# Attention with two mixture layers: row scaling on two engines, a branch ahead of the row loads, full-width transposes

## The chip, the cores and the metric

The kernel runs on one core of a Trainium2 chip. A core has TensorE (PE, matrix products, its weight loads listed as PEld), VectorE (DVE), ScalarE (ACT), GpSimd (POOL) and SyncE (SP, which here only issues DMAs and reads registers). The metric is the device time of one execution in microseconds (us).

## The reference

Three layers follow one another on B = 4, H = 8, S = 576, D = 64 (2304 tokens, 512 channels):

```python
scores = scale * np.matmul(q, k.transpose(0, 1, 3, 2))
bias = -(cum[:, :, :, None] - cum[:, :, None, :])          # cum: running sum of max(s, 0)
scores = np.where(causal, -1000000000.0, scores + np.minimum(bias, 0.0))
attn = softmax(scores);  x = attn @ v                       # to 2304 x 512
...
logits = xn @ en.T / tau;  expert_idx = np.argmax(logits, axis=1)   # 8 experts, normed rows
out[mask] = gate_w[mask, None] * (np.maximum(x[mask] @ w1[e], 0.0) @ w2[e])   # 512 -> 1024 -> 512
...
return (x @ w_a) * (x @ w_b) @ w_out                        # 512 -> 1536 -> 512
```

## The kernel before

**Attention (0 to 262 us).** The 32 heads are worked in units. A planner, class `Sched` (object `V`), keeps a time for each of four engines (P, A, D, G) and a heap of follow-up operations; `run` takes, among several streams of PE items, the one that can start first by the planner's costs, emits its matmuls, and `push` and `chain` put the evictions, maxima, exponentials and copies on the engines. Where `push` names two engines it takes the one that would end first. The order that results is fixed in the program. The streams are the scores (`s_item`, `s0_item`), transposes of the exponentials (`t_item`), products with v (`a_item`), and, per tile of 128 tokens, `x_item`, `l_item` and `r_item`. There are 20 tiles, five per batch; the last one (t = 19) has 64 tokens.

`x_item` multiplies attention's output by the router's embedding (L857, tile `lp`, logits with experts in rows), and transposes it into rows of tokens (L862, tile `pt`); DVE scales the rows by the reciprocal row sums (`fx`, L895, into `x`), ACT squares them (`fs`, L902, into `ss`), and the logits are copied to `lt`. `l_item` transposes `lt` back (L930), DVE finds the largest (L938 to L953) and makes the one-hot row `oh` (L956), and GpSimd keeps a running sum `sc` (L961). `r_item` gets each token's rank within its expert by products of `oh` with a triangle (L982) and of `sc` with ones (L983), and GpSimd scatters the rows to the sorted buffer `xs` by indirect DMA (L1004).

**Handover.** The counts are summed on PE (L1250), copied (L1257), sorted on DVE and written as integers to `ci` (L1274). Then come base offsets (L1276 to L1281), twelve operations that split three loaded weight tiles into a high and a low half (`hi_op` on ACT, `lo_op` on DVE, L280), and the gate's pieces m1 to m4 (L1443 to L1458) on DVE. SP, having waited for all scatters, loads the first expert's rows (`xload(0)`, L1332 and L1333, tile `xg`) and a weight tile (`wload2`, L242). PE runs 30 warm-up matmuls on a weight tile (L174, count in `WARM[2]`). All engines then read the number of tokens above capacity from `ci` (L1719) and branch around `overflow()` (L1661), which serves experts above their capacity and is not entered with these counts. `xtr0` transposes the rows (L1345); ACT makes `xh`, DVE `xl` (L1349).

**Experts (about 273 to 500 us).** The eight experts stand in order of their counts, with fixed capacities 352, 368, 344, 328, 296, 288, 288, 272. For each f of eight, PE makes `h` (L1510) from `xh` and `xl` and `y` (L1535) from the split `hh` and `hl` (L1518, L1519). `xtr` transposes the next expert's rows, a third of them m = capacity - 256 wide (L1361). The results go to `yt` (L1547); `yload` (L1580) reads 384 of its columns for the last layer, `ysplit` splits them (L1587, L1588).

**Last layer (about 500 us to the end).** Six groups of 384 tokens; `abmm` (L1600), `omm` (L1621). Its weights arrive as 64-bit values, decoded on ACT, DVE (L254 to L265) and split (L1431, L1433) in steps called ticks.

Of the kernel before, what the change touches and what calls it, by code (L numbers as in the profile page):

```python
# [35 lines left out]
WARM = (30, 84, 30, 0, 20, 28)  # L36
# [108 lines left out]
def moe_kernel(tc, q, k, v, s, emb, tau, w1, w2, wa, wb, wo, out, dbg=None):  # L145
# [36 lines left out]
    with left, right:  # L182
# [23 lines left out]
        ci = rt.tile([1, 5, E], I32, name="ci")  # L206
        tie = rt.tile([128, E], F32, name="tie")
# [80 lines left out]
        if True:  # L288
# [293 lines left out]
            def start(i):  # L582
# [84 lines left out]

            def s0_item(i):
# [12 lines left out]
                def emit(end):  # L681
# [22 lines left out]
                    def th1(t):  # L704
                        rel.t = t
                        V.push(t, "A", 0.833 * 64 + 280, f2, lambda t2: setattr(et, "t", t2))
# [132 lines left out]

            def x_item(b, c):  # L840
# [11 lines left out]
                def emit(end):  # L852
# [3 lines left out]
                    for p in range(NP):  # L856
                        nc.tensor.matmul(  # L857
                            lp[32 * p:32 * p + 32, :m], lhsT=enbd[:, p].rearrange("p h e -> p (h e)"),
                            rhs=xtt[4 * b + p][:, s0:s0 + m], start=True, stop=True,
                        )  # L860
# [5 lines left out]
                    r = sm.tile([128, H], F32, name="r")  # L866
                    lt = sm2.tile([128, 128], F32, name="lt")
# [8 lines left out]
                    def f0a(_):  # L876
                        if c:
                            nc.vector.tensor_scalar(out=r[:m], in0=rsum[:m, t, :], scalar1=1e-9, scalar2=None, op0=ALU.add)
                        for h in range(0 if c else 2):
                            nc.vector.tensor_scalar(  # L880
                                out=r[:m].rearrange("p (a h) -> p a h", h=2)[:, :, h],
                                in0=rsum0[64 * h:64 * h + 64, NP * b:NP * b + NP],
                                scalar1=1e-9, scalar2=None, op0=ALU.add,
                            )
# [7 lines left out]
                    V.push(end - 400, "DA", (dt(m), at(m)), f0, th)  # L892
# [10 lines left out]

                    def thx(t_):
                        rel.t = t_
                        V.push(t_, "A", 620, fs)

                    rk_ = rtok[t] = Tok()

                    def thr(t_):  # L910
                        rk_.t = t_
                        V.push(max(t_, end), "D", dt(512), fx, thx)
# [7 lines left out]
            def l_item(b, c):  # L920
# [6 lines left out]
                def emit(end):  # L927
                    x, r, lt = rts[t]
                    lp = ps_t.tile([128, 512], F32, name="pt")
                    nc.tensor.transpose(out=lp[:m, :128], in_=lt[:, :m], identity=ident)  # L930
                    rel = Tok()
                    pts.append(rel)
# [898 lines left out]
```

## Time and profile before

| | |
|---|---|
| median of three runs | 963.38 us (962.12 to 964.65) |
| profiled execution | 960.65 us, of which 959.0 are the profile's span |
| PE busy | 925.7 us, 97% of the span |
| PEld, DVE, ACT, POOL busy | 846.6, 514.6, 432.8, 255.1 us |
| data moved | 107.90 MB, mean 113 GB/s |

The profile's chain of work that ended last lies on PE for 66% of the span, on DVE and on DMA for 2% each. PE's pieces are pipelined and their ends are modelled, so how close PE is to its limit is read from the distance of starts, not from its share.

### The profile page before, as it was taken

The page shows a single profiled execution, that of the slowest core. Times are in us where ns is not written, and L with a number is a line of the kernel's source. Part 1 is how long each engine was busy: PE and PEld are TensorE (multiplying, and loading weights), DVE is VectorE, ACT ScalarE, POOL GpSimd, SP SyncE. Part 2 cuts the span into 40 slices and gives each one's busy share as a digit, 9 for nine tenths or more (in the row PEclk, how much of TensorE's full clock was granted, in tenths as well). Part 3 has the DMA queues.
Part 4 walks back from the last instruction along what each step waited for, and adds up shares of the span by engine and source line. Part 5 has one row for each costly group of instructions (what it writes and reads, how often), then busy time and mean ns, then how long its engine had stood idle before and what let it go on. Part 6 is the DMA issues. An engine that isn't in the chain of part 4 may idle for free.

```text
span 959.0 us, 17720 instructions
## 1 busy us (share of the span) xinstructions
PE 925.7 (97%) x6471; PEld 846.6 (88%) x6472; DVE 514.6 (54%) x1319; ACT 432.8 (45%) x1075; POOL 255.1 (27%) x311
## 2 busy tenths in 40 slices
PE   8999999999889999999999999999999999999996
PEld 7777778777779999999998999999999999999995
DVE  8688889798764334444558888742222212222112
ACT  6677788876745444455544444432211211211111
POOL 6122323256223333344302433642001001001001
PEclk9999999999999999999999999999999999999999
DMA  4774555526286667667645443613010010000000
GB/s 130 172 155 110 137 119 124 139 71 183 72 254 227 225 192 231 201 211 222 190 156 166 132 132 119 108 18 100 1 33 34 1 33 33 1 1 33 1 1 33
DMA packets 102243, 107.90 MB, mean 113 GB/s; under 512 B 58429, under 2 KB 72717, under 8 KB 102141
## 3 DMA queue, kind: packets, MB, share of 16 engines
q1 hardware_dynamic: 98557, 97.04, 36.2%
q0 software_dynamic: 3552, 9.46, 2.8%
q8 instruction: 65, 1.06, 0.5%
q14 instruction: 37, 0.30, 0.1%
q10 hardware_dynamic: 32, 0.04, 0.0%
HBM read 77.90 MB, written 20.44 MB: 103 GB/s over the span
## 4 chain that ended last, share of the span: by engine, by line
PE 66%; DVE 2%; DMA 2%; issue 1%; ACT 0%; POOL 0%; POOLq 0%; SPq 0%; DVEq 0%; ACTq 0%
PE h L1600 15%; PE x L1600 15%; PE y L1621 13%; PE h L1510 11%; PE y L1535 10%; PE x L1361 1%; DMA xg<-xs 1%; PE x L1621 1%; PE h L1621 1%; DMA xg<-yt 1%; DVE cv L262 0%; DVE cv L265 0%; DVE mx L1611 0%; DVE w L1433 0%; DVE xl L1588 0%
## 5 line engine op out<-in xcount | busy, mean ns | idle before, releaser
L1611 DVE TENSOR_TENSOR mx<-x,mx 128x384 f32<-128x384 f32 x72 | 40.0, 556 | 220.0 <-PE x L1600 220.0
L1612 ACT CAST hh<-mx 128x384 fp32r<-128x384 f32 x71 | 36.4, 513 | 161.1 <-DVE mx L1611 161.1
L1606 ACT COPY mx<-h 128x384 f32<-128x384 f32 x72 | 34.6, 481 | 144.1 <-PE h L1600 144.1
L650 ACT ACTIVATE z<-z,mn 128x192 f32<-128x192 f32 (+3 forms) x128 | 78.2, 611 | 37.8 <-DVE mn L644 37.2
L1640 POOL DMA_INDIRECT out_dram<-mx,pmt x18 | 17.6, 979 | 291.0 <-DVE mx L1639 221.7
L1600 PE MATMUL x<-xh,w 128*128 128x384 f32 x288 | 79.0, 335 | 1.0 <-POOL w L1433 1.0
L1600 PE MATMUL h<-xh,w 128*128 128x384 f32 x288 | 79.7, 337 | 0.0
L1600 PE MATMUL h<-xh,v 128*128 128x384 f32 x288 | 79.7, 337 | 0.0
L630 PE MATMUL st<-KS,QS 128*128 128x288 f32 (+3 forms) x160 | 58.6, 374 | 8.9 <-DVE mn L644 7.5
L738 PE MATMUL pt<-ident,z 128*128 128x128 f32 x448 | 63.4, 277 | 3.2 <-ACT pT L180 1.6
L1519 DVE SCALAR_TENSOR_TENSOR hl<-h,hh 128x288 fp32r<-128x288 f32 (+6 forms) x64 | 31.2, 488 | 65.1 <-ACT hh L1518 65.1
L280 POOL TENSOR_TENSOR w<-st,w 128x512 fp32r<-128x512 f32 (+1 forms) x41 | 44.5, 1093 | 74.2 <-ACT w L272 48.9
L644 DVE CUSTOM_DVE_ANT_0 z<-st,maskb 128x192 f32<-128x192 f32 (+3 forms) x128 | 58.7, 478 | 9.5 <-PE st L633 7.6
L782 PE MATMUL xa<-pT,vn 128*64 128x128 f32 x896 | 61.2, 282 | 0.8 <-ACT pT L180 0.4
L1613 DVE TENSOR_TENSOR hl<-mx,hh 128x384 fp32r<-128x384 f32 x71 | 39.7, 559 | 41.1 <-ACT hh L1612 41.1
L1621 PE MATMUL y<-v,hh 128*128 128x512 f32 x192 | 59.8, 392 | 0.0
L280 POOL TENSOR_TENSOR v<-st,v 128x512 fp32r<-128x512 f32 x32 | 42.9, 1341 | 63.3 <-ACT v L272 53.0
L738 PEld LDWEIGHTS pt<-ident,z 128*128 128x128 f32 x448 | 49.8, 141 | 11.0 <-ACT z L650 4.3
L1510 PE MATMUL h<-xh,v 128*128 128x256 f32 (+2 forms) x256 | 59.2, 305 | 0.0
L1510 PE MATMUL h<-xh,w 128*128 128x288 f32 (+3 forms) x256 | 58.9, 306 | 0.0
L1535 PE MATMUL y<-hh,v 128*128 128x256 f32 (+2 forms) x256 | 58.1, 300 | 0.0
L782 PEld LDWEIGHTS xa<-pT,vn 128*64 128x64 f32 x896 | 49.1, 139 | 9.9 <-issue 5.7
(299 smaller groups left out, 2525.7 us busy)
## 6 DMA issues: line engine op xcount, KB each, us to landing
st<-in_moe_w_dram SPq DMA_DIRECT2D x64, 512.0 KB
QS<-sp SPq DMA_DIRECT2D x62, 128.0 KB
st<-in_moe_w_a_dram SPq DMA_DIRECT2D x12, 512.0 KB
st<-in_moe_w_b_dram SPq DMA_DIRECT2D x12, 512.0 KB
st<-in_moe_w_out_dram SPq DMA_DIRECT2D x12, 512.0 KB
xg<-yt SPq DMA_DIRECT2D x6, 768.0 KB
xg<-xs SPq DMA_DIRECT2D x8, 512.0 KB
kn<-in_k_dram SPq DMA_DIRECT2D x24, 128.0 KB
```

Source lines behind the costliest of these rows:

```text
L280: e.tensor_tensor(out=o[:, 1, a:b], in0=t[:, a:b], in1=o[:, 0, a:b].bitcast(F32), op=ALU.subtract)
L630: nc.tensor.matmul(st[:m, :wp], lhsT=qs[:, h, s0 - 64:s0 - 64 + m], rhs=ks[:, h, c0:c0 + wp], start=True, stop=False)
L644: nc.vector.tensor_tensor_reduce(out=z[:m, h, c0:c0 + w], in0=st[:m, :w], in1=maskb[:m, S - kk + c0:S - kk + c0 + w], op0=ALU.add, op1=ALU ...
L650: nc.scalar.activation(out=z[:m, h, :kk], in_=z[:m, h, :kk], func=AF.Exp, scale=-1.0, bias=m1, accum_out=rsum[:m, tid(b, c), 2 * p + h:2 * ...
L738: nc.tensor.transpose(out=pt[:, 128 * x:128 * x + 128], in_=zs[i][:, h, a0:a0 + 128] if c else z0s[u % 2], identity=ident)
L782: nc.tensor.matmul(xa[64 * h:64 * h + 64, :m], lhsT=v_[:m, 2 * p + h, :], rhs=locs[i][bk, h], start=bk == 0, stop=bk == c,)
L1510: nc.tensor.matmul(ph[:, :n], lhsT=w[:, hl, 128 * f:128 * f + 128], rhs=mv[:, d, :n], start=k_ == 0, stop=k_ == 11,)
L1535: nc.tensor.matmul(ys[e][d][:, :n], lhsT=w[:, hl, c0 + 128 * d:c0 + 128 * d + 128], rhs=mv[:, :n], start=f == 0 and k_ == 0, stop=f == 7 a ...
L1600: nc.tensor.matmul(p, lhsT=w[:, hl, d, c0:c0 + 128], rhs=mv[:, d, :], start=d == 0 and k_ == 0, stop=d == 3 and k_ == 2,)
L1611: nc.vector.tensor_tensor(out=g, in0=pp[1], in1=g, op=ALU.mult)
L1613: nc.vector.tensor_tensor(out=gl, in0=g, in1=gh.bitcast(F32), op=ALU.subtract)
L1621: nc.tensor.matmul(ots[i][t], lhsT=st[:, 128 * t:128 * t + 128], rhs=w[:, hl, c0:c0 + 512], start=f == 0 and k_ == 0, stop=f == 11 and k_ ...
```

## The change

- The tiles of batches 0 to 2 may be scaled by DVE as before (`fx`), or copied by ACT (`fy`) and multiplied by GpSimd (`fm`); the planner picks. By the order of the program, 16 of the 20 scalings stay on DVE; of batch 1 and of batch 2 the 64-token tile and one of 128 tokens go the other way.
- The last tile's logits are computed with tokens in rows, so it has no `lt` copy and no transpose; its reciprocal (`rlast`) is made early, and its scaling comes behind its one-hot row.
- The running sum `sc` ends five tiles early; `r_item` and the final count add products of `oh` with ones in its place.
- `cov`, an integer copy of the overflow counts, is made right behind their maximum; branch and `overflow()` stand ahead of `xload(0)`, which is now three loads of at most 128 rows. One `wload2` goes ahead of the branch. The low halves of three weight tiles go behind it, a third of them on GpSimd. Of m1 to m4 two stay ahead of `xtr0`; base offsets go into m5.
- `WARM`: 30 matmuls ahead of the branch become 2 ahead and 3 behind, and 28 in the last `r_item` become 10.
- The third transpose of each row tile is always 128 x 128.
- `yload(0)` goes from the last expert's f = 1 to the f = 7 before; a tick is added in the last expert at f = 5, with fewer loads ahead from f = 4.
- The zeroing of the first rows of `xs` moves from a list of pending loads to a fixed place, unit step 14.

```diff
-WARM = (30, 84, 30, 0, 20, 28)
+WARM = (30, 84, 2, 0, 20, 10, 3)
...
+                if i == 14:
+                    zero(xs[:CAPS[0], :], 0)
...
+                        if t == NT - 1:
+                            nc.tensor.matmul(lp[:m, 32 * p:32 * p + 32], lhsT=xw, rhs=ew, start=True, stop=True)
+                        else:
+                            nc.tensor.matmul(lp[32 * p:32 * p + 32, :m], lhsT=ew, rhs=xw, start=True, stop=True)
...
+                    def fy(e):
+                        on[0] = e
+                        if e == "D":
+                            fx(e)
+                        else:
+                            nc.scalar.copy(out=x[:m], in_=pt[:m])
+
+                    def fm(_):
+                        nc.gpsimd.tensor_tensor(
+                            out=x[:m].rearrange("p (h d) -> p h d", h=H), in0=x[:m].rearrange("p (h d) -> p h d", h=H),
+                            in1=r[:m].unsqueeze(2).to_broadcast([m, H, D]), op=ALU.mult,
+                        )
...
-                        V.push(max(t_, end), "D", dt(512), fx, thx)
+                        if b < B - 1:
+                            V.push(max(t_, end), "DA", (dt(512), at(512)), fy, thx)
+                        else:
+                            V.push(max(t_, end), "D", dt(512), fx, thx)
...
-                        V.push(t_, "G", 163, f7, lambda t2: setattr(ot, "t", t2))
+                        if t == NT - 1:
+                            more(t_)
+                        if t < NT - 5:
+                            V.push(t_, "G", 163, f7, lambda t2: setattr(ot, "t", t2))
...
+                    for x in range(a, t0):
+                        nc.tensor.matmul(rp[:, :w], lhsT=ones, rhs=oh[:, x, :], start=False, stop=False)
...
+            nc.vector.tensor_copy(out=cov, in_=over[:1])
...
                     hi_op("A", wstate[j], slots["s", j], a, a + 512)
-                    lo_op("D", wstate[j], slots["s", j], a, a + 512)
...
                 if e == 0:
-                    for x in ld:
-                        behind("xs", x)
+                    nc.vector.memset(t[96:, 2], 0.0)
+                if e == 0:
+                    for a in range(3):
+                        m = min(128, CAPS[0] - 128 * a)
+                        behind("xs", nc.sync.dma_start(out=t[:m, a], in_=xs[128 * a:128 * a + m, :]))
+                    return
...
-                    m = min(128, cap - 128 * a)
                     nc.tensor.transpose(
-                        out=pt[:, 128 * a:128 * a + m], in_=xgs[e][:m, a, 128 * d:128 * d + 128], identity=ident[:m, :m]
+                        out=pt[:, 128 * a:128 * a + 128], in_=xgs[e][:, a, 128 * d:128 * d + 128], identity=ident
                     )
...
+            wload2()
+            idle(WARM[2])
+            most = nc.values_load(cov[:1, 0:1], min_val=-CAP, max_val=N)
+            overflow()
             xload(0)
-            wload2()
-            for _ in range(4):
-                misc.pop(0)()
...
+            idle(WARM[6])
             count(0)
-            most = nc.values_load(ci[:1, 2, 0:1], min_val=-CAP, max_val=N)
-            overflow()
+            for j in range(4, 7):
+                for x in range(2):
+                    lo_op("DG"[j == 6], wstate[j], slots[0, j], 512 * x, 512 * x + 512)
+            for _ in range(2):
+                misc.pop(0)()
...
-                    if (e, f) == (E - 1, 1):
+                    if (e, f) == (E - 2, 7):
                         yload(0)
...
-                        for _ in range(TICKS[0] if f not in (4, 5, 6) else 0):
-                            tick(5 if f < 7 else 3)
+                        for _ in range(TICKS[0] if f not in (4, 6) else 0):
+                            tick(5 if f < 4 else 3)
```

The first place is SP at the handover, before: `st` are weight loads, `xg<-xs` the first expert's rows, L1719 and L1661 the read and the branch of the overflow.

```order
L242 DMA st<-in_moe_w_dram 128x2x512 x3
L1332 DMA xg<-xs 128x2x512
L1333 DMA xg<-xs 96x512
L242 DMA st<-in_moe_w_dram 128x2x512
L1711 TENSOR_LOAD ci
L1711 ISA x2
L1320 TENSOR_LOAD ci
L1320 ISA x2
L1719 TENSOR_LOAD ci
L1719 ISA x2
L1661 COMPARE_AND_BRANCH
```

After, the same engine; L1725 is the branch, and what stands inside the overflow is left out.

```order
L243 DMA st<-in_moe_w_dram 128x2x512 x4
L1781 TENSOR_LOAD cov
L1781 ISA x2
L1725 COMPARE_AND_BRANCH
...
L1393 DMA xg<-xs 128x512 x2
L1393 DMA xg<-xs 96x512
L1784 TENSOR_LOAD ci
```

The row loads moved from ahead of the branch to behind it, and the fourth weight load from behind the rows to ahead of both.

The second place is DVE at the handover, before: L280 are the low halves, L1443 to L1458 m1 to m4.

```order
L1274 CAST ci<-pk 1x40
L1276 TENSOR_TENSOR lw<-pk,iota_85 128x64
L1280 TENSOR_TENSOR lw<-lw,pk 128x64
L1281 TENSOR_REDUCE base<-lw 128x8
L280 TENSOR_TENSOR w_4050<-st,w_4050 128x512 x2
L280 TENSOR_TENSOR w_4128<-st,w_4128 128x512 x2
L280 TENSOR_TENSOR w_4159<-st,w_4159 128x512 x2
L1443 TENSOR_SCALAR nr<-nr 128x20
...
L1458 TENSOR_TENSOR pd<-gm 128x20
L1719 TENSOR_LOAD ci
L1661 COMPARE_AND_BRANCH
```

After:

```order
L1339 CAST ci<-pk 1x40
L1781 TENSOR_LOAD cov
L1725 COMPARE_AND_BRANCH
...
L1389 MEMSET xg 32x512
L281 TENSOR_TENSOR w_4055<-st,w_4055 128x512 x2
L281 TENSOR_TENSOR w_4133<-st,w_4133 128x512 x2
L1500 TENSOR_SCALAR nr<-nr 128x20
L1501 RECIPROCAL nr<-nr 128x20
L1504 TENSOR_TENSOR lt<-lg,nr 128x160
L1505 TENSOR_REDUCE gm<-lt 128x20
L1506 TENSOR_TENSOR lt<-lt,gm 128x160
L1407 TENSOR_TENSOR xl<-y_4637,xh 128x256
```

The branch moved ahead of all low halves; two of six and the last four of m1 to m4's operations no longer stand ahead of `xl`.

The third place is SP in the last two experts, before: `st` are the last layer's weights, `yt<-mx` an expert's results, `xg<-yt` the last layer's first input.

```order
L248 DMA st_8763<-in_moe_w_b_dram 128x2x512
L1494 UNCONDITIONAL_BRANCH x2
L248 DMA st_8823<-in_moe_w_b_dram 128x2x512
...
L1547 DMA yt<-mx 128x288
L248 DMA st_8900<-in_moe_w_out_dram 128x1024
L1580 DMA xg<-yt 128x4x384
```

After:

```order
L249 DMA st_8734<-in_moe_w_b_dram 128x2x512
L1644 DMA xg<-yt 128x4x384
L1558 UNCONDITIONAL_BRANCH x2
L249 DMA st_8796<-in_moe_w_b_dram 128x2x512
...
L1611 DMA yt<-mx 128x288
L249 DMA st_8873<-in_moe_w_out_dram 128x1024
```

The input's load moved ahead of one weight load, an expert's four stores and another weight load.

## Rows read from the trace of the kernel before

**Rows 1.** Windows of 24 us: busy us (instructions) of PE, PEld, DVE, ACT, POOL; clock, DMA share, GB/s.
```profile
264.00:288.00 24.00, 19.92 (x124) 17.89 (x123) 15.70 (x36) 10.30 (x25) 6.12 (x8) 0.93 0.82 258
...
480.00:504.00 24.00, 23.06 (x176) 22.86 (x176) 14.29 (x29) 9.94 (x24) 0.00 (x0) 1.00 0.44 152
...
528.00:552.00 24.00, 24.00 (x129) 22.60 (x129) 20.01 (x25) 10.03 (x20) 9.85 (x6) 1.00 0.43 130
```

**Rows 2.** Timeline of DVE, handover: start us, us, instruction, tiles, count, [idle before <-releaser].
```profile
259.84 0.17 DVE L1257 COPY c<-pt 128x8 f32<-128x8 f32 x1
...
262.62 0.17 DVE L1274 CAST ci<-pk 1x40 int32<-1x40 f32 x1
...
263.62 3.70 DVE L280 TENSOR_TENSOR w<-st,w 128x512 fp32r<-128x512 f32 x6 [0.18 <-issue]
...
268.47 0.33 DVE L1449 TENSOR_TENSOR lt<-lt,gm 128x160 f32<-128x160 f32 x1
...
271.51 2.46 DVE L1349 TENSOR_TENSOR xl<-y,xh 128x256 fp32r<-128x256 f32 x8 [1.27 <-DVEq L1661]
```

**Rows 3.** Timeline of SP, handover: the first load of rows.
```profile
263.04 0.37 SPq L1332 DMA_DIRECT2D xg<-xs  x1
```

**Rows 4.** Timeline of PE, handover.
```profile
270.21 1.06 PE L1345 MATMUL y<-ident,xg 128*128 128x128 f32 x8 [2.90 <-PEq L1661]
...
273.12 0.60 PE L1510 MATMUL h<-xh,w 128*128 128x288 f32 x1
```

**Rows 5.** Instructions of L1661: ns min/median/max, first and last start us.
```profile
L1661 PEldq COMPARE_BRANCH x1: 5480/5480/5480, 264.4 to 264.4; - x1
```

**Rows 6.** DMA traffic from 262 to 270 us, in 40 slices of 0.2 us.
```profile
GB/s 246 0 0 0 0 0 0 0 0 0 102 92 82 72 246 369 348 430 369 328 358 369 297 205 328 358 225 307 389 338 389 246 21 0 10 10 31 20 10 0
```

**Rows 7.** Windows of 2 us, columns as in the first group (the clock is third from the end).
```profile
272.00:274.00 2.00, 1.96 (x8) 1.47 (x9) 1.77 (x7) 0.96 (x4) 0.00 (x0) 0.62 0.66 150
274.00:276.00 2.00, 2.00 (x10) 2.00 (x10) 0.00 (x0) 0.00 (x0) 0.00 (x0) 0.53 0.93 186
```

**Rows 8.** Timeline of PE where a third transpose has 72 rows.
```profile
346.96 0.44 PE L1361 MATMUL x<-ident,xg 128*128 128x128 f32 x3
...
347.44 0.31 PE L1510 MATMUL h<-xl,w 128*128 128x336 f32 x1
347.59 0.47 PE L1510 MATMUL h<-xh,w 128*128 128x336 f32 x2
```

**Rows 9.** Timeline of PE where a third transpose has 32 rows.
```profile
436.57 0.55 PE L1361 MATMUL x<-ident,xg 128*128 128x128 f32 x3
...
437.27 0.28 PE L1510 MATMUL h<-xl,v 128*128 128x256 f32 x1
437.39 0.41 PE L1510 MATMUL h<-xh,v 128*128 128x256 f32 x2
```

**Rows 10.** Timeline of PE in the last expert.
```profile
489.31 0.39 PE L1535 MATMUL y<-hl,v 128*128 128x256 f32 x1 [0.94 <-DVE hl L1519]
```

**Rows 11.** Timeline of DVE in the last expert.
```profile
485.80 0.56 DVE L1588 TENSOR_TENSOR xl<-xg,xh 128x384 fp32r<-128x384 f32 x1 [2.19 <-ACT xh L1587]
```

**Rows 12.** Timeline of SP in the last expert.
```profile
479.04 0.64 SPq L1580 DMA_DIRECT2D xg<-yt  x1
```

**Rows 13.** Timeline of PE in the last layer's first group.
```profile
525.87 0.62 PE L1600 MATMUL x<-xh,w 128*128 128x384 f32 x2 [0.97 <-POOL w L1433]
```

**Rows 14.** Timeline of POOL in the last layer's first group.
```profile
524.09 1.72 POOL L1433 TENSOR_TENSOR w<-cv,w 128x512 fp32r<-128x512 f32 x1 [2.73 <-ACT w L1431]
```

**Rows 15.** Waits of PE, 60 to 246 us: us in total, times, longest.
```profile
PE st L630 <- DVE mn L644: 5.1, 13, 0.8
```

**Rows 16.** Attention's groups by line: shapes, count | busy us, mean ns | idle before <-releasers.
```profile
L895 DVE TENSOR_TENSOR x<-pt,r 128x512 f32<-128x512 f32 x16 | 11.0, 689 | 1.5 <-PE pt L862 0.6 <-PE pt L983 0.2
...
L540 POOL CAST KS<-KH 64x576 fp32r<-64x576 f32 x32 | 21.8, 682 | 74.3 <-ACT KH L407 72.2 <-DMA xs<-x,sl 1.2
...
L180 ACT COPY pT<-pt 128x512 f32<-128x512 f32 x72 | 40.3, 580 | 5.6 <-PE pt L738 5.1
```

More of the change, by code (lines that the diff above doesn't have):

```diff
@@ L206, in moe_kernel @@
         ci = rt.tile([1, 5, E], I32, name="ci")
+        cov = rt.tile([1, E], I32, name="cov")
         tie = rt.tile([128, E], F32, name="tie")
@@ L666, in s_item @@
                 return (need, 2 * wp / 2.4 + 10, emit)
+            n0 = [0]
             def s0_item(i):
@@ L705, in th1, with th2, f3 @@
                         rel.t = t
-                        V.push(t, "A", 0.833 * 64 + 280, f2, lambda t2: setattr(et, "t", t2))
+                        V.push(t, "A", 0.833 * 64 + 280, f2, th2)
+                    def th2(t):
+                        et.t = t
+                        n0[0] += u > last - NP
+                        if n0[0] == NP:
+                            rlast[0] = sm.tile([128, H], F32, name="r")
+                            def f3(_):
+                                for h in range(2):
+                                    first_r(rlast[0], B - 1, h)
+                                nc.vector.reciprocal(out=rlast[0][:64], in_=rlast[0][:64])
+                            V.push(t, "D", 560, f3)
                     V.push(end, "D", 1.042 * 64 + 77, f1, th1)
@@ L879, in f0a @@
                         for h in range(0 if c else 2):
[L880 to L884, printed above, removed]
+                            first_r(r, b, h)
                     def f0b(_):
@@ L928, in emit @@
                     x, r, lt = rts[t]
[L929 to L932, printed above, removed]
+                    if t == NT - 1:
+                        lp, (rel, more) = lt, lend[0]
+                    else:
+                        lp = ps_t.tile([128, 512], F32, name="pt")
+                        nc.tensor.transpose(out=lp[:m, :128], in_=lt[:, :m], identity=ident)
+                        rel = Tok()
+                        pts.append(rel)
                     lw = sm3.tile([128, H, E], F32, name="lw")
@@ L1249, in moe_kernel @@
             pt = ps_t.tile([128, 512], F32, name="pt")
-            nc.tensor.matmul(pt[:, :E], lhsT=ones, rhs=sc[:, NT, :], start=True, stop=True)
+            nc.tensor.matmul(pt[:, :E], lhsT=ones, rhs=sc[:, NT - 5, :], start=True, stop=False)
+            for t in range(NT - 5, NT):
+                nc.tensor.matmul(pt[:, :E], lhsT=ones, rhs=oh[:, t, :], start=False, stop=t == NT - 1)
             sbase, scnt, over, perm, more = (pk[:, x] for x in range(5))
```

82 lines of the change are left out of this document (49 added, 33 removed).

## The prediction

> **What bounds the kernel now.** I read the 24-us windows first, for the stretches where TensorE (PE) isn't full, and then, inside those, the timelines of the engine that ended the wait last. From about 276 us on PE is busy all of the time, as in the last row of [rows 1], except in two windows that each lack about 1 us; the first of them is the row with 23.06, the other holds the stall of [rows 13]. So behind 276 us only PE's own instructions and two stalls are worth anything. The stretch between attention and the experts is the one real hole: 19.92 of 24 [rows 1]. In attention (0 to 262 us) PE idles in many small pieces; the largest cause from 60 to 246 us is a wait for VectorE's row maximum, 5.1 us in 13 pieces [rows 15]. The profiled execution took 960.65 us, 2.73 under the median of 963.38; I work out differences in it and take them from the median.
>
> **Handover, the largest term.** The reader should see a chain on VectorE (DVE) and one on the row loads, meeting at the first `xl`. Before: counts copied at 259.84, `ci` ready at 262.79 (262.62 + 0.17), six low halves of 3.70 us together until 267.3, m1 to m4 until 270.25, then the branch, 1.27 us, and `xl` at 271.51 [rows 2]. PE's branch alone took 5.48 us [rows 5], while 704 KB of rows and 512 KB of weights came in [rows 6]; PE resumed at 270.21 after 2.90 us of idling and began the expert matmuls (L1510) at 273.12 [rows 4], 1.61 us behind the first `xl`.
> After, on DVE: the last tile's scale (0.69) goes from ahead of its one-hot to behind it, which the counts don't gain by; its logits lose a copy and a transpose; and no running sum on GpSimd is waited for. I put the counts' copy 0.3 us earlier, at 259.5 (bounds 0 and 0.7; no row prices the chain as a whole). To `ci` it is 2.95 us plus one more small copy of 0.17 (`cov`): 262.6. Branch 1.27: 263.9. Four of the six low halves, 3.70 x 4/6 = 2.5, and a small memset, 0.1: 266.5. m1 and m2 took from 267.32 to 268.80, 1.5 us: 268.0 [rows 2]. The other two low halves go to GpSimd, m3 and m4 into the first expert, base/eq into m5, all beside PE's work of many microseconds; if that cover were gone they would cost DVE about 3 us again.
> After, on the load's side: `cov` is ready six small operations ahead of `ci`; at 0.17 each, as `ci`'s own [rows 2], that is 1.0 us: 261.6. SP's read and branch I price like DVE's passage, 1.27: issue at 262.9, against 263.04 before, where SP was released by the last scattered rows [rows 3]. So the wait is no longer only for the scatters, but the branch fits beside it. What is queued behind SP's branch is only these three loads and the weights after them. The w2 load goes ahead of the branch into a buffer whose last readers are the attention scores, so it is gone before the one-hots. Before, bytes flowed in full from 264.8, 1.75 us behind the first issue, to 268.4 us, at about 330 GB/s [rows 6]; 704 KB alone need 2.2 us of that. So 262.9 + 1.75 + 2.2: landed at about 266.8, with transposes and the first `xh` some 0.8 us more: 267.6. DVE's 268.0 is later and sets `xl`: 3.5 us earlier than 271.51.
> PE gives some of it back. The clock stood at 0.62 and 0.53 in the two windows from 272 to 276 [rows 7], that is near its level of 1.2 GHz, (0.38 + 0.47) x 2 = 1.7 us of work lost, and that after thirty warm matmuls that kept PE busy until 267.3. Now five are left, and PE is nearly idle from about 260 to 266.8. I let half clock start with the transposes and last into the expert as long as before, and charge 0.5 us more. The Trainium skill, "TensorE: Matmul & The Clock Gate", section "What's actually happening", says that the throttled level is the default and that activity lifts it; it speaks against taking warm matmuls away, and the rows agree that the level falls behind an idle PE; what it would do here is rival A. Handover: -3.0 us, bounds -4.2 and +0.5.
>
> **Transposes in full width.** Of the 28 places L1361 in the experts, those of the four smallest experts (40, 32, 32 and 16 rows in the third transpose, 16 places) widen across 64 rows. At a place with 72 rows, from the first transpose to the second L1510 it is 0.48 us; less one pitch of 0.15 that leaves 0.33 for three transposes, 0.11 each [rows 8]. At one with 32 rows it is 0.70, less 0.12: 0.58 [rows 9]. The narrow third costs 0.25 us more than a wide one. Those with 72 to 112 rows behave like the first place, so widening them gives nothing, nor does the 96-row one of the first expert. 16 x 0.25 = 4.0 us, all on PE, which is full: -4.0, bounds -4.4 (0.27 each) and 0 (rival B). The copies behind them read the same columns as before. The Trainium skill, "TensorEngine Tiling (Array Packing)", section "Instruction Overhead", gives each matmul a fixed cost of about 60 cycles, below which a small free size saves nothing; by this alone 128 columns instead of 32 cost 68 cycles more, at 2.4 GHz an estimated 0.03 us each, and the sum would be 16 x 0.03 = +0.5 instead of -4.0. The rows contradict it here: the narrow one is the dearer [rows 8, 9].
>
> **Two stalls.** At 489.31 PE waited 0.94 us for `hl` [rows 10]. DVE had idled 2.19 us until 485.80 for the first second-stage input [rows 11], loaded by an issue at 479.04 [rows 12], and its backlog delayed `hl`. The load now goes ahead of the second w_b load and of the four result stores on SP, some 7 us or more earlier; the idle time goes and with it the stall: -0.9. It takes 768 KB from the weights' transfers there, which are not needed before the second stage. At 525.87 PE waited 0.97 us for a low half on GpSimd that ran from 524.09 for 1.72 us [rows 13, 14]. An additional tick in the last expert has the decoding one item ahead: -0.9, bounds -1.0 and +0.5 (the tick adds DVE work to an expert that already stalls; its own idle 2.19 us covers it).
>
> **Attention.** By the order only four of the fifteen tiles of the first three batches leave DVE. That takes 4 x 0.69 = 2.8 us from DVE, adds 4 copies of about 0.58 to ScalarE and 4 products to GpSimd at up to 1.72 us [rows 14, 16]. PE's 5.1 us of waits for DVE [rows 15] is all that this can reach, and the new plan moves other things with it: -0.3, bounds -1.5 and +1.5. The zeroing of the first rows moves five issues later on SP, long before anything is scattered: 0. Ten more tiny matmuls for ranks stand where PE waits: 0.
>
> **Sum:** -3.0 - 4.0 - 0.9 - 0.9 - 0.3 = -9.1, so 963.4 - 9.1 = **954.3 us** (the profiled execution near 951.6).
>
> **Rivals.** A: the handover gives nothing. SP's branch could miss like PE's (5.48 instead of 1.27), so the loads go out some 3 us later, or PE's longer idle time keeps the clock at half 3 us longer (1.5 us) with the load chain 1.5 late. For it: [rows 5, 7]; against: PE's long branch stood behind 1.2 MB of loads, and DVE's short one did not. 954.3 + 3.0 = 957.3. The rule of the Trainium skill on the clock gate, cited above, points this way.
> B: the change doesn't do what it says in the experts: the 0.25 us of [rows 9] is the switch to the following wide matmul or the copy's wait, and stays, so full width saves nothing: 954.3 + 4.0 = 958.3. Against it: the same neighbours stand around [rows 8], without the 0.25. By the rule of the Trainium skill's tiling page, cited above, it would be 958.8.
> C: the two stalls stay, because the input is late for another reason or the tick only moves the queue: 954.3 + 1.8 = 956.1.
> D, slower: GpSimd now multiplies rows in front of the casts of `KS` that the next unit's scores need. Each of the four products (1.72) then holds PE, and each hold is followed by half clock as at the handover (1.7): 4 x 3.4 = 13.7, so 954.3 + 13.7 = 968.0, +4.6. It decides once GpSimd reaches `KS` later than ScalarE hands over `KH`. Against it: GpSimd idled 72.2 us in front of these casts, waiting for ScalarE [rows 16].
>
> **How the numbers follow.** Forecast 0.60, A 0.15, B 0.08, C 0.11, D 0.06. The forecast's own range: the good ends of handover (1.2), attention (1.2) and transposes (0.4) together give 951.5; the bad end of attention (1.8) and a stall that stays (0.9) give 957.0. A to C reach 958.3. The median of three itself lay 1.3 from its ends (962.12 to 964.65); half of that, 0.7, goes on at either side: 950.8 to 959.0, which leaves out D and the cases in which two things fail at once, 2 in 10 at most. A difference of 0.3%, 2.9 us, is about what can be told from no change, so faster is below 960.5 and slower above 966.3. Faster: 0.60 + 0.15 + 0.11 with a little of each lost to two mishaps at once, and most of B: 0.86. Same 0.08. Slower 0.06 (D).
>
> **What would show it.** The first `xl` near 268 and L1510 near 269.6; half clock no longer than to about 273; 0.33 us at every L1361 place; no wait of PE near 489 and 525; attention ending within 1.5 us of before. Wrong if the row loads are issued later than 264, or if the third transpose still costs 0.25 more.

## The result and the profile after

| | before | changed |
|---|---|---|
| median, us | 963.56 (962.12 to 964.65, 4 runs) | 955.58 (954.86 to 955.97, 4 runs) |
| ratio to before | | 0.9917, interval 0.9900 to 0.9934 |
| profiled execution (span), us | 960.65 (959.0) | 955.97 (954.3) |

The forecast was 954.3 in a range of 950.8 to 959.0; the time lies in it, 1.3 us above the forecast. But the pair of profiles is only 4.7 us apart, where the medians are 8.0 apart, and the largest term of the forecast, the handover, did not come. The sum was near because two terms were larger than forecast and because of 3.3 us that the pair of profiles doesn't contain. So the nearness of the total is in part luck, and that was worth taking apart.

First the windows of 24 us, as in [rows 1] (start and end; length; busy us of PE, PEld, DVE, ACT, POOL; clock, DMA share, GB/s):

```profile
264.00:288.00 24.00, 18.55 (x105) 14.42 (x104) 12.92 (x26) 11.20 (x24) 8.35 (x6) 0.93 0.67 206
...
480.00:504.00 24.00, 24.00 (x175) 23.78 (x175) 17.70 (x36) 11.89 (x27) 0.00 (x0) 1.00 0.34 107
504.00:528.00 24.00, 23.91 (x126) 22.02 (x126) 20.61 (x28) 10.79 (x21) 9.42 (x6) 1.00 0.59 191
```

The hole between attention and experts has become larger (PE busy for 18.55 of 24, before 19.92); the two windows with a stall are full, or nearly so (24.00 and 23.91). The timeline of DVE at the handover answers [rows 2] (start us, us, engine line op, tiles, count, idle before and releaser):

```profile
260.38 0.16 DVE L1321 COPY c<-pt 128x8 f32<-128x8 f32 x1
...
263.23 0.17 DVE L1339 CAST ci<-pk 1x40 int32<-1x40 f32 x1
265.11 0.48 DVE L1389 MEMSET xg<- 32x512 f32 x1 [1.70 <-DVEq L1725]
265.62 3.11 DVE L281 TENSOR_TENSOR w<-st,w 128x512 fp32r<-128x512 f32 x4
...
269.88 0.32 DVE L1506 TENSOR_TENSOR lt<-lt,gm 128x160 f32<-128x160 f32 x1
273.62 1.58 DVE L1407 TENSOR_TENSOR xl<-y,xh 128x256 fp32r<-128x256 f32 x5 [3.42 <-ACT xh L1406]
```

DVE is free at 270.2, forecast 268.0, and then waits 3.42 us for `xh`, which ScalarE makes from the transposed rows: not DVE but what stands ahead of the transposes sets `xl`, at 273.62 instead of 271.51. The timeline of SP, for [rows 3]:

```profile
267.58 2.17 SPq L1393 DMA_DIRECT2D xg<-xs  x3
273.34 0.66 SPq L1278 DMA_DIRECT2D xs<-zrow  x1
274.21 4.64 SPq L243 DMA_DIRECT2D st<-in_moe_w_dram  x4
279.64 0.39 SPq L1395 DMA_DIRECT2D xg<-xs  x1
```

The first row load goes out at 267.58, not at 262.9 as forecast; 7.20 us behind the counts' copy, before 3.20. PE, for [rows 4]:

```profile
267.29 3.57 PE L174 MATMUL h<-w 128*128 128x512 f32 x4 [3.11 <-PEq L1725]
270.70 1.02 PE L174 MATMUL y<-w 128*128 128x512 f32 x2
271.56 0.27 PE L1403 MATMUL y<-ident,xg 128*128 128x128 f32 x1
272.81 0.99 PE L1403 MATMUL y<-ident,xg 128*128 128x128 f32 x7 [0.98 <-DMA xg<-xs]
...
275.23 0.39 PE L1574 MATMUL h<-xh,w 128*128 128x288 f32 x1
```

The three warm matmuls (L174) hold PE from 267.29 to 271.56; only the transposes behind the first one then wait for rows, 0.98 us. The expert matmuls begin at 275.23, 2.1 us later than before. The time in front of that, on SP and PE, is in the instructions of the register read ahead of the branch, L1781 (count; ns min/median/max; first and last start):

```profile
L1781 SPq TENSOR_LOAD <-cov x1: 688/688/688, 262.5 to 262.5; - x1
```

and of the branch itself, L1725, for [rows 5]:

```profile
L1725 SPq EVENT_SEMAPHORE  x9: 17/17/17, 266.6 to 267.2; - x9
...
L1725 PEldq COMPARE_BRANCH x1: 3642/3642/3642, 263.3 to 263.3; - x1
...
L1725 SPq COMPARE_BRANCH x1: 50/50/50, 263.6 to 263.6; - x1
```

From SP's compare at 263.6 to its next event (an instruction that only waits for or sets a semaphore) at 266.6 are 3.0 us. In the kernel before it was 3.6 us, with loads in flight:

```profile
L1661 SPq EVENT_SEMAPHORE  x9: 17/17/17, 270.1 to 270.7; - x9
...
L1661 SPq COMPARE_BRANCH x1: 50/50/50, 266.5 to 266.5; - x1
```

The DMA view of the changed kernel from 264 to 266 us shows what moved meanwhile:

```profile
DMA packets 3, 0.03 MB, mean 16 GB/s; under 512 B 0, under 2 KB 0, under 8 KB 0
...
q8 instruction: 1, 0.02, 3.6%
q14 instruction: 2, 0.02, 2.6%
```

Three packets of instructions and nothing else. So the passage is slow with empty queues too. PE's branch took 3.64 us here and 5.48 before [rows 5]. Over all twelve profiles it is 5.0 to 6.0 us in the three kernels with the branch of before, 3.4 to 3.9 in the others, those with the rows ahead of the branch included; that the loads in flight made the difference is likely, not shown.

A ledger of the pair of profiles, by the starts of the same instructions (after less before): the counts' copy +0.54; from there to the second expert's first matmul +1.07 (41.63 against 40.56); from that to the last expert's first -4.00; the last expert -1.20; the last layer -1.12. Together -4.7.

### The profile page after: what moved, and what is told of

It reads as the page before. It is cut to its first block, busy times and chain, and to the rows that moved or that the text cites. A ratio compares the mean times of both kernels' runs of the same rounds, so it can differ in the third digit from the quotient of the medians.

```text
span 954.3 us, 17686 instructions
## 1 busy us (share of the span) xinstructions
PE 920.2 (96%) x6447; PEld 842.6 (88%) x6448; DVE 518.4 (54%) x1320; ACT 432.3 (45%) x1073; POOL 259.9 (27%) x312
## 4 chain that ended last, share of the span: by engine, by line
PE 68%; DMA 2%; DVE 1%; issue 0%; SPq 0%; POOLq 0%; ACT 0%; DVEq 0%; ACTq 0%
PE h L1664 16%; PE x L1664 15%; PE y L1685 14%; PE y L1599 10%; PE h L1574 10%; DMA xg<-xs 1%; PE x L1418 1%; PE x L1685 1%; PE h L1685 1%; DMA xs<-zrow 1%; DVE xl L1652 0%; SPq L1393 0%; POOLq L1899 0%; DVE cv L266 0%; DVE mx L178 0%
## 5 line engine op out<-in xcount | busy, mean ns | idle before, releaser
L281 POOL TENSOR_TENSOR w<-st,w 128x512 fp32r<-128x512 f32 (+1 forms) x43 | 47.0, 1101 | 69.0 <-ACT w L273 58.8
```

The source lines that it names most:

```text
L281: e.tensor_tensor(out=o[:, 1, a:b], in0=t[:, a:b], in1=o[:, 0, a:b].bitcast(F32), op=ALU.subtract)
```

## The experiments

Timed differences here are of the size of attention's spread from run to run, so each experiment is read by the lengths of its stages too. They are taken from starts of the same instructions in each trace, in us: the counts' copy (line `nc.vector.tensor_copy(out=cnt...)`), from there to the first row load, to the first `xl` and to the second expert's first matmul, from there to the last expert's first, from the last expert's first `h` matmul to its last (the column "8th"), and the last layer's `abmm` matmuls, first to last.

| kernel | counts | to row load | to `xl` | to 2nd expert | 2nd to 8th | 8th | last layer |
|---|---|---|---|---|---|---|---|
| before | 259.84 | 3.20 | 11.68 | 40.56 | 171.85 | 22.68 | 447.77 |
| changed | 260.38 | 7.21 | 13.25 | 41.63 | 167.85 | 21.48 | 446.65 |
| after_again | 260.46 | 6.80 | 11.94 | 40.10 | 167.85 | 21.48 | 447.59 |
| full_width_alone | 265.26 | 3.24 | 12.44 | 41.58 | 167.85 | 23.73 | 447.76 |
| input_early_alone | 261.00 | 3.19 | 12.02 | 40.78 | 171.85 | 21.48 | 447.75 |
| scaling_on_vector | 259.25 | 6.98 | 12.33 | 40.83 | 167.84 | 21.48 | 446.65 |
| branch_first_no_warm | 267.72 | 6.69 | 11.94 | 40.22 | 168.06 | 21.48 | 454.88 |
| rows_ahead_of_branch | 263.95 | 3.20 | 13.30 | 40.03 | 167.85 | 21.48 | 456.69 |
| rows_ahead_no_warm | 262.98 | 3.22 | 9.55 | 40.15 | 167.85 | 21.48 | 454.71 |
| fill_early_rows_ahead | 259.93 | 3.70 | 9.75 | 38.74 | 168.06 | 21.48 | 446.65 |
| combined | 259.17 | 3.68 | 9.74 | 37.70 | 167.84 | 21.48 | 447.32 |
| combined_warm | 259.51 | 3.68 | 9.74 | 37.86 | 167.84 | 21.48 | 446.63 |

Four of them (full_width_alone, branch_first_no_warm, rows_ahead_of_branch and rows_ahead_no_warm) ran on a chip on which the kernel before took 970.16 us (966.71 to 974.54). Their counts come 2 to 8 us later than elsewhere, and in all but the first the last layer is 8 to 10 us longer, with waits of PE between 600 and 650 us; no edit explains either. Their totals say little, and the changed kernel was not timed on that chip; the stages between the counts and the last layer agree with the other profiles.

### The full width alone

```diff
 # the kernel before, xtr; the unused rows of the first tile are set to zero once
-                    m = min(128, cap - 128 * a)
                     nc.tensor.transpose(
-                        out=pt[:, 128 * a:128 * a + m], in_=xgs[e][:m, a, 128 * d:128 * d + 128], identity=ident[:m, :m]
+                        out=pt[:, 128 * a:128 * a + 128], in_=xgs[e][:, a, 128 * d:128 * d + 128], identity=ident
                     )
```

> The kernel before with one part of the change: the third transpose of every later expert in full width (and the unused rows of the first expert's tile set to zero once). Theory (a transpose over 64 rows or fewer costs PE 0.25 us more than a full one, at 16 places): 4.0 us less than before, 0.996 of it, and 0.33 us at every place. Rival (the 0.25 us belongs to what stands behind the third transpose): no difference, and still 0.58 us at the places of the four smallest experts.

Measured: 968.64 against 970.16 us, ratio 0.9981 (0.9962 to 0.9999). From the second expert to the last it takes 167.85 us instead of 171.85: 4.00 us less, to the hundredth what the first profile of the changed kernel has there. PE's timeline at a place that had 32 rows before, to be set beside [rows 9]:

```profile
440.72 0.49 PE L1362 MATMUL x<-ident,xg 128*128 128x128 f32 x3
...
441.17 0.28 PE L1511 MATMUL h<-xl,v 128*128 128x256 f32 x1
441.28 0.40 PE L1511 MATMUL h<-xh,v 128*128 128x256 f32 x2
```

441.17 - 440.72 is 0.45, less a pitch of 0.11: 0.34, as for 72 rows. The theory stands, and the rival falls: the 0.25 us belongs to the narrow shape. The total moved by 1.5 us and not by 4.0, since a stall behind it grew. The waits of PE from 480 to 530 us (us in total, times, longest):

```profile
PE y L1536 <- DVE hl L1520: 1.7, 1, 1.7
PE x L1601 <- POOL w L1434: 1.0, 1, 1.0
```

The wait for `hl` was 0.94 [rows 10] and is now 1.7; the last expert takes 23.73 instead of 22.68. PE comes to the late input earlier and waits longer. That takes back 1.05 us; the 2.9 us left lie within the total's interval (0.1 to 3.7 us). The full width needs the earlier input to keep all of its 4 us.

### The input early, alone

```diff
 # the kernel before
-                    if (e, f) == (E - 1, 1):
+                    if (e, f) == (E - 2, 7):
                         yload(0)
```

> The kernel before with only the load of the last layer's first input two steps earlier. Theory: VectorE's wait of 2.2 us for the input and PE's wait for hl near the last expert's f = 5 vanish, the last expert's matmuls take 21.5 instead of 22.7 us, and PE's wait for the low half on GpSimd in the first group, 1.0 us, stays, so that it belongs to the added tick. Rival (the weights' transfers that now stand behind the input come late instead): the first wait goes, another of about 1 us comes in the last layer.

Measured, in a single run: 960.8 us beside 963.24 (959.38 to 965.28), which tells nothing by itself. The last expert takes 21.48 us, and of PE's waits from 480 to 530 us one is left:

```profile
PE x L1600 <- POOL w L1433: 1.0, 1, 1.0
```

The theory stands. The load removes the stall of [rows 10]; the one of [rows 13] stays and so belongs to something else in the change. That it is the added tick is argued from [rows 14], since no run has the tick alone. In the changed kernel neither stall is there, without any new one. The first gain is 1.20 us, not 0.94: the 0.94 counts from the modelled end of the matmul before, 0.28 us behind its start, where the usual pitch is 0.12, and the first matmul behind the stall takes 0.23 instead of 0.12.

### The branch and the row loads

```diff
 # the changed kernel: rows_ahead_of_branch; rows_ahead_no_warm has the second edit as well,
 # branch_first_no_warm the second alone
             wload2()
+            xload(0)
             idle(WARM[2])
             most = nc.values_load(cov[:1, 0:1], min_val=-CAP, max_val=N)
             overflow()
-            xload(0)
...
-WARM = (30, 84, 2, 0, 20, 10, 3)
+WARM = (30, 84, 2, 0, 20, 10, 0)
```

> The changed kernel with the three row loads ahead of the branch again, all else as changed. Theory (SP's passage through the branch takes 3 us from compare to release even with no loads in flight, and now stands ahead of the loads): the first row load is issued near 264, as soon as the scatters have landed, instead of 267.6, and the rows land near 268; PE, held by the three warm matmuls until about 271.6, starts the transposes there instead of 272.8: 1.2 us less than the changed kernel. Rival (the scatters land late and the loads would have waited for them anyway): issue near 267, no difference.

Measured: 967.87 against 970.16 us, 0.9976 (0.9959 to 0.9993). The first row load goes out 3.20 us behind the counts' copy, as in the kernel before, against 7.21 and 6.80 in two profiles of the changed kernel. So the scatters had long landed and it was the branch that held the rows: 3.6 to 4.0 us. The rival falls. But the expected 1.2 us did not come: `xl` is as late as in the changed kernel (13.30 against 13.25 and 11.94), since the three warm matmuls, here all at half clock, held PE, which the next run takes away:

> As the run with the row loads ahead of the branch, and without the three warm matmuls behind it. Theory (those matmuls, in plain fp32 and at half clock 1.1 to 1.8 us each, are what holds PE once the rows come early): transposes from about 268, the first xl when VectorE is free near 270.2 instead of 273.6, so 3.4 us sooner than the changed kernel, of which a half-clock stretch in the first expert takes back up to 1.7: 1.7 to 3.4 us less than the changed kernel. Rival (the warm matmuls are worth their time by the clock): no gain over the run with them.

Measured: 967.93 against 970.16 us, 0.9977 (0.9959 to 0.9996). `xl` now comes 9.55 us behind the counts, 3.7 us sooner than in the changed kernel's profile and 2.1 sooner than before, about as the theory had it. And yet the second expert starts at 40.15, before 40.56, changed 41.63 and 40.10, so the expected gain of 1.7 to 3.4 us did not come. It is given back inside the first expert, and half clock is only a part of it. PE's waits from 280 to 300 us:

```profile
PE x L1418 <- DMA xg<-xs: 1.7, 2, 1.3
```

It is the second expert's rows that come late. In the changed kernel they did so as well:

```profile
287.54 0.41 PE L1418 MATMUL x<-ident,xg 128*128 128x128 f32 x2 [1.00 <-DMA xg<-xs]
```

SP's timeline of the changed kernel above shows why. The zero-fill of the second expert's unused rows (L1278, 273.34) waits until the first expert's rows have landed, since both touch `xs` (SP waits 2.0 us for that); the second expert's rows (L1395, 279.64) wait until the fill has landed. The chain of work that ended last, in that stretch, has the pieces (start us, us, what):

```profile
269.33 3.81 DMA xg<-xs
...
273.34 6.19 DMA xs<-zrow
...
280.27 7.85 DMA xg<-xs
```

Nearly 19 us of transfers one behind another, next to some 11 us of PE's work from 275.23 on: this second chain sets the second expert's start. Moving the first rows ahead of the branch doesn't shorten it. In rows_ahead_no_warm the fill waits for no rows any more, but goes out 11.19 us behind the counts all the same (before 11.30, changed 12.96, after_again 11.54):

```profile
266.20 2.19 SPq L1393 DMA_DIRECT2D xg<-xs  x3
274.17 0.66 SPq L1278 DMA_DIRECT2D xs<-zrow  x1
...
280.48 0.39 SPq L1395 DMA_DIRECT2D xg<-xs  x1
```

SP now has the three issues, the branch (2.5 us from its compare at 269.3 to its next event at 271.9) and two register reads in front of the fill, one behind another. So the fill goes out at 11.2 to 13.0 in both orders, the second expert's rows 6.3 us behind it, and a first matmul that starts earlier only waits longer for them.

> The changed kernel without the three warm matmuls behind the branch. Theory (PE waits for the rows until 272.8 anyway, and the three matmuls only bring the clock back): transposes start at the same time but at half clock, which lasts some 3.4 us into the first expert: 1.3 to 1.7 us more than the changed kernel. Rival (the clock comes back in the same time): no difference.

Measured: 968.18 against 970.16 us, 0.9971 (0.9953 to 0.9989). The theory fails: the second expert starts at 40.22, not later than in the changed kernel (41.63 and 40.10), and the total is that of the two runs with the rows ahead. The clock was at its lower level far into the first expert, as the 2-us windows of that kernel show (clock third from the end):

```profile
278.00:280.00 2.00, 1.39 (x7) 1.30 (x7) 0.34 (x1) 0.73 (x2) 0.00 (x0) 0.50 0.27 102
...
282.00:284.00 2.00, 2.00 (x10) 2.00 (x10) 0.26 (x1) 0.13 (x1) 0.00 (x0) 0.50 0.92 182
```

In the changed kernel it was back at 272:

```profile
270.00:272.00 2.00, 1.83 (x5) 0.65 (x3) 0.21 (x1) 0.00 (x0) 0.00 (x0) 0.86 0.73 225
272.00:274.00 2.00, 0.99 (x7) 0.75 (x7) 0.38 (x2) 0.78 (x3) 0.00 (x0) 1.00 0.02 5
```

So with the warm matmuls the clock is back earlier here (at 1.00 from 272 on, 11.6 us behind the counts, against 0.50 until 284, 16.3 us behind them), and it is worth nothing, since the second expert's rows decide (their fill goes out at 11.65). In rows_ahead_of_branch the same three matmuls ran at 0.50 to their end. The expectation failed by the same omission as the forecast.

### The scaling

```diff
 # the changed kernel
-                            V.push(max(t_, end), "DA", (dt(512), at(512)), fy, thx)
+                            V.push(max(t_, end), "D", dt(512), fy, thx)
```

> The changed kernel with all row scalings on VectorE as before; ScalarE's copies and GpSimd's products are gone, the rest of the change stands, and the planner orders attention anew. Theory (the four moved scalings reach nothing, since PE's waits for the row maximum grew from 5.1 to 6.8 us with them): attention ends within 0.7 us of the changed kernel, and the total is the same within 0.3%. Rival (moving them is a gain that the new order hides): attention ends 1 to 3 us later.

Measured: 956.42 (954.01 to 956.91), ratio 0.9928 (0.9904 to 0.9953), beside 956.56 for the changed kernel in the same series: the same. Its profile copies the counts at 259.25, the changed kernel's two at 260.38 and 260.46. About 0.65 us of this is older than the first moved tile (at 136.67 us): from 24 to 33 us both profiles of the changed kernel had a longer stretch of half clock (granted 0.63, 0.50 and 0.73 in three windows of 3 us), and a stretch like it stands in the kernel before too, shorter (0.95, 0.50 and 0.98). Some 0.5 us is left for the moved scalings, against them. The waits of PE from 60 to 246 us, changed kernel, for [rows 15]:

```profile
PE st L633 <- DVE mn L647: 6.8, 11, 1.2
```

and with all scalings on VectorE:

```profile
PE st L633 <- DVE mn L647: 5.1, 13, 0.8
```

The waits for the row maximum that the four scalings were to relieve grew with them and go back without them. A loss of up to 0.5 us is likely, no gain is seen; the total can't tell it.

### The control

> The changed kernel unaltered, against the kernel before on the same chip. Theory (the stages that changed are the same in every run, and the rest of the spread is attention's own): behind the first expert the lengths of the profile recur to 0.1 us (experts 2 to 8 without the last: 167.85 against 171.85 us; the last expert's matmuls 21.48 against 22.68; the last layer 1.1 shorter), the branch again puts 6.5 to 7.5 us between the counts' copy and the first row load, and the total is 4 to 8 us less than before. Rival (the 8 us between the medians stand on the luck of the four runs): less than 3 us.

Measured: 956.56 (953.35 to 959.88, 7 runs) against 963.24 (959.38 to 965.28, 11 runs), 0.9931 (0.9906 to 0.9957): 6.7 us. The stages behind the first expert recur to 0.01 us, apart from one wait of 1.2 us in the last layer; so does the late row load (6.80). The handover was 1.5 us shorter than in the first profile of the same program (40.10 against 41.63), so a difference of that size in it means nothing from one profile. The second chain tells where it comes from: the last of the first rows took 2.72 us to land instead of 3.81, and the fill behind them went out 11.54 us behind the counts instead of 12.96.

### A version that beats both

```diff
 # the changed kernel with rows_ahead_no_warm's edits, and:
                 if i == 14:
                     zero(xs[:CAPS[0], :], 0)
+                if 16 <= i < 30 and i % 2 == 0:
+                    x = i // 2 - 7
+                    zero(xs[x * RW + 256:x * RW + 368, :], None)
...
-            zfill(1)
```

`zero` with None fills 112 rows. The second expert isn't known yet in attention, so the rows from 256 on are filled for all seven.

> The changed kernel with the row loads ahead of the branch, without the three warm matmuls, and with the zeroing of the second expert's unused rows done for all experts in attention (112 rows each) instead of between its two row loads; rows of 256 and more only, which serves these counts. Theory (a second chain sets the first expert's end: rows landed, zero-fill 6.2 us, second expert's rows, their transposes): the second expert's rows are loaded 2 us or more sooner, PE's wait of 1.2 to 1.7 us for them goes, and from the counts' copy to the second expert's first matmul it takes 38 to 39 us instead of 40.2 (without the early fill) and 41.6 (changed kernel); in all 2 to 3 us less than the changed kernel. Rival (PE's half clock and the weights in the queues set it): 40 us as without the early fill.

Measured: 952.06 (951.24 to 952.98), ratio 0.9882 (0.9850 to 0.9914), against 956.56 for the changed kernel in the same series. The timeline of SP:

```profile
263.63 2.63 SPq L1396 DMA_DIRECT2D xg<-xs  x3
271.77 2.15 SPq L243 DMA_DIRECT2D st<-in_moe_w_dram  x4
274.18 0.74 SPq L1398 DMA_DIRECT2D xg<-xs  x1
```

and PE at the second expert's first transposes, without a wait:

```profile
284.69 0.49 PE L1421 MATMUL x<-ident,xg 128*128 128x128 f32 x3
```

The second expert's rows go out 14.25 us behind the counts' copy, in the changed kernel 19.26 and 17.83, and the second expert starts at 38.74. In this and the next two runs, which all fill early, it starts at 37.70 to 38.74; in the six other profiles with the change's branch at 40.03 to 41.63. The second chain was the bound, and with it off the path the earlier `xl` is worth 1.4 us and more. The version needs counts of 256 or more for all experts, which a finished kernel would have to secure.

```diff
 # combined: fill_early_rows_ahead and scaling_on_vector; combined_warm besides:
-            w = slots[0, 0][:, 0, :].bitcast(F32)
+            w = slots[0, 0][:, 0, :]
...
-WARM = (30, 84, 2, 0, 20, 10, 0)
+WARM = (30, 84, 12, 0, 20, 10, 3)
```

> The run with the early fill and the rows ahead of the branch, with all row scalings on VectorE besides. Theory (the two gains stand in different stages and add): the counts are copied 0.5 to 1.1 us sooner than with the moved scalings, the stretch from there to the second expert stays at 38.7 us, and the total is 2.5 to 4 us less than the changed kernel, 0.987 to 0.989 of the kernel before. Rival (attention's spread covers it): the same as the run with the early fill.

> As the combined run, with warm-up matmuls in the one-pass type of the kernel before: twelve ahead of the branch (3 us at full clock) and three behind it. Theory (the 10 us of half clock from 266 to 276 take some 2 us from the first expert, and PE stands idle there only because the matmuls were left out): the half-clock stretch shrinks to 3 to 7 us and the second expert starts up to 1.5 us sooner. Rival (PE idles some 4 us in the branch whatever stands ahead of it, so the clock falls as before; or the second expert's rows set its start): no difference.

Measured: combined 951.71 (949.29 to 952.20), 0.9874 (0.9839 to 0.9909); combined_warm 950.86 (949.27 to 951.34), 0.9866 (0.9832 to 0.9899). Stage by stage the gains add (counts at 259.17, second expert at 37.70), but against the run with the early fill alone, 0.9882, the intervals overlap. The stretch to the second expert was expected to stay at 38.7. The clock goes with the difference: in combined it stood at 1.00 in the window from 274 to 276, in the run with the early fill alone at 0.50 until 276. With the chain off the path the clock may well count, though no run shows that alone. The warm matmuls shortened the half clock further, as the windows of combined_warm show:

```profile
270.00:272.00 2.00, 2.00 (x13) 1.65 (x12) 1.53 (x7) 0.91 (x4) 0.00 (x0) 0.81 0.00 0
272.00:274.00 2.00, 2.00 (x18) 2.00 (x17) 0.78 (x2) 1.27 (x3) 0.00 (x0) 1.00 0.78 283
```

But PE then waited 0.8 us for the second expert's rows again, and 37.86 against 37.70 is no gain. Both are the fastest of this study, at 11.6 and 12.5 us under the kernel before (963.31 in their series).

## Why the prediction was right, and where it was not

- **Sign and range** were right: 0.9917, within the range, 1.3 us above the forecast.
- **Transposes in full width**, -4.0: right, -3.8 to -4.0 in every trace that has them. The rows of the changed kernel at the place of [rows 9]:

```profile
435.89 0.49 PE L1418 MATMUL x<-ident,xg 128*128 128x128 f32 x3
...
436.34 0.28 PE L1574 MATMUL h<-xl,v 128*128 128x256 f32 x1
436.46 0.40 PE L1574 MATMUL h<-xh,v 128*128 128x256 f32 x2
```

0.45 less 0.12 is 0.33, as 72 rows had. The fixed cost of a matmul, by which the widening would have lost, is not what decides. The Trainium skill, "TensorEngine Tiling (Array Packing)", section "Key Properties", says that a change of the tiling mode drains the engine. The traces fit it (112, 88 and 72 rows 0.33 us a place, 40, 32 and 16 rows 0.57 to 0.60), though no view shows which mode a transpose took; the forecast should have named it as the likely reason. What was not foreseen is that alone the gain is partly lost again in the stall at the last expert.
- **Two stalls**, -1.8: right in mechanism (the tick's part argued), and larger, 1.20 and 1.12 us, since an idle time that counts from a modelled end is less than the stall costs. VectorE took up the input without the idle time of [rows 11], loaded at 467.33 instead of 479.04.
- **Attention**, -0.3: wrong in sign in the profiles, +0.54 at the counts' copy, within its bounds. About 0.65 of it is the clock early on, some 0.5 the moved scalings, and the shorter tail of the last tile gave some 0.6 back (from the last full score matmul to the counts' copy 14.2 us, before 14.8).
- **Handover**, -3.0: this failed, and by the prediction's own sign (row loads later than 264). Three steps of it failed:
  - The first is "SP's read and branch I price like DVE's passage, 1.27": it took 5.1 us from the read at 262.5 to the first load at 267.58, of which 3.6 to 4.0 us held the rows (rows_ahead_of_branch). Rival A named just this, gave it 0.15, and argued against it that PE's long branch stood behind loads. That argument holds for 1.8 of PE's 5.48 us at most and for nothing of SP's. The row that should have been read was SP's own in the kernel before: its compare at 266.5 and its next event at 270.1, 3.6 us, shown above and in the same view as [rows 5]. DVE's own passage, 1.70, and a low half that took 1.31 instead of 0.68 while GpSimd ran the other two cost DVE some 1.0 us more, hidden behind the late rows.
  - The second is a term put at nothing: the three warm matmuls behind the branch, which held PE from 267.29 to 271.56. Even rows in time would have met a busy PE, and in rows_ahead_of_branch they did: the rows went out 3.6 to 4.0 us earlier, and `xl` came at 13.30 (13.25 and 11.94 in the changed kernel).
  - The third is an omission. "What is queued behind SP's branch is only these three loads and the weights after them" leaves out the zero-fill and the second expert's rows, and "DVE's 268.0 ... sets `xl`: 3.5 us earlier" was booked as a gain of the whole kernel, without following what the first expert waits for next. The fill stands behind SP's branch in either order and, in the changed kernel, behind the first rows too. rows_ahead_no_warm shows that `xl` earlier by 2.1 us than before is worth 0.4 while this chain stands, and fill_early_rows_ahead that it was the bound.
- **Clock**, +0.5: wrong in detail. The clock was back (1.00 from 272 on) before the first expert, behind the three matmuls, so that before's loss in 274 to 276 went away; it was worth nothing, since the chain on SP decided.
- **What makes up the rest.** By the parts that the profiles show, the change is worth 4.7 us; the medians say 8.0 and, in the control, 6.7. The profile of the kernel before, 960.65, lies 2.9 us under its median, that of the changed kernel 0.4 above its own. Attention alone ended between 259.84 and 261.00 us in the two profiles with the order of before that are not from the slower chip. Which stage of the kernel before is longer in its usual run is not shown, since a timed run leaves no trace; it stays open. By the profiles alone the forecast of -9.1 would have been nearly twice the 4.7 measured, and nearly all of the difference stands at the handover.

## What to carry to other kernels

When a step is moved ahead of a load, price the passage with that queue's own rows, not with another engine's; a passage that took VectorE 1.3 us took SP 5. When a start is made earlier, follow the next input of the same kind too: its chain (here load, zero-fill, load) may set the end, and on a queue that also branches it stands behind the branch wherever the first load goes. What is put in to keep the clock up has a length of its own and is priced like any other work. And a gain on the full engine can be eaten by the next late input, so two edits that look separate may only pay together.

## What the runs showed of the hardware

- From the compare of the branch to the engine's next event, with no load in flight: at most 0.2 us on ScalarE and on GpSimd, 0.6 on VectorE, 3.0 on SP, 3.7 on PE, with three instruction packets in the queues. Over all twelve profiles SP took 2.5 to 3.6 us. Why SP takes nearly as long as PE is not settled.
- Two transposes of 128 columns and one of 16 to 40 take 0.57 to 0.60 us to the matmul behind them, three of 128 columns 0.33.
- A subtraction of 128x512 on VectorE took 1.31 us while GpSimd ran one of its own, and 0.68 right after it (the group of four took 3.11 us, of six without GpSimd 3.70 [rows 2]). GpSimd's two, and the first of VectorE's:

```profile
263.89 2.49 POOL L281 TENSOR_TENSOR w<-st,w 128x512 fp32r<-128x512 f32 x2 [1.76 <-POOLq L1725]
```

```profile
265.62 1.31 DVE L281 TENSOR_TENSOR w<-st,w 128x512 fp32r<-128x512 f32 x1
```

The Trainium skill, "GPSIMD Engine Reference", section "Specifications", names such contention for VectorE instructions with two inputs in SBUF; the rows agree, with this one overlap.
